# Four units to a burst, PSUM in three double slots and two single banks, and an earlier x: a fused attention and channel-mix kernel

## The chip, the cores and the metric

The kernel runs on one core of a Trainium2 chip. TensorE (PE) multiplies matrices into PSUM, VectorE (DVE), ScalarE (ACT) and GpSimd (POOL) work on tiles, and SyncE (SP) issues transfers. Each engine takes its instructions in the order in which they are written and waits for the others by semaphores. The metric is the time of one execution on the device, in microseconds; of several runs the median counts. Inputs are those of the reference, except that the channel mix's weights and factors arrive as float64.

## The reference

Two pieces follow each other on x of shape (4, 12608, 128). First an attention through 32 inducing points: the points attend to all of x, which gives h (32 rows for each batch), and each row of x attends to h. Then a channel mix, with d_ff = 1024, in which each row is mixed with the row before it:

```python
def mab(q, kv):
    s = scale * (q @ kv.transpose(0, 2, 1))
    s = s - s.max(-1, keepdims=True)
    a = np.exp(s)
    a /= a.sum(-1, keepdims=True) + 1e-09
    return a @ kv
h = mab(I, x)
x = mab(x, h)
...
x_prev = np.concatenate([np.zeros((B, 1, D)), x[:, :-1, :]], axis=1)
xk = mu_k * x + (1.0 - mu_k) * x_prev
xr = mu_r * x + (1.0 - mu_r) * x_prev
k = np.maximum(xk @ w_k, 0.0)
v = k * k @ w_v
r = 1.0 / (1.0 + np.exp(-(xr @ w_r)))
out = r * v
```

## The kernel before

**Tiling.** A batch is cut into six blocks of 2048 tokens and a tail of 320, a block into four groups of 512 tokens; with the tail's, a batch has 25 groups. A group's 1024 channels of d_ff are cut into four units of 256. So there are 100 groups and 400 units, and the main loop goes through them, one unit to an iteration. The second attention's normalised weights (not its output rows) stand in `R`, as a high and a low part, and the kernel multiplies them with `h @ w_k` and `h @ w_r`, made once for each batch by `combine`; so the up product of a unit has an inner length of 64 and runs as pairs of half-height matmuls.

**One unit.** `up` (six half-height matmuls in three pairs, L792) fills a double slot of PSUM. `square` then takes relu on VectorE (L802, to `k_t`), the square rounded to `kh` on ScalarE (L807), or on VectorE for the units of the set `high_vector` (L804), the full square on ScalarE (L808), and the rest `kl` as a difference on GpSimd (L810). `down` (L821) multiplies `kh` and `kl` with `w_v` in six full-height matmuls, four units later (`LAG`). Once a group, `zgate` (L780) makes the sigmoid gate, `gate` (L826) multiplies, `store` (L837) transposes and sends out.

**The other stages.** Between the units stand the steps of the attention. `stage_a` brings one block of the next batch through the first attention: transposes on VectorE (L344) whose parts SP copies into place (L347), scores, maximum, exponentials, their transpose (L420), sums (L430) and a product with x (`hmm`, L441), added to a running sum (L456). `stage_b` brings the next block of this batch through the second: scores (L621), maximum, exponentials, total (L642, L643), reciprocal (L646), multiplication (L649), a transpose back (L655, L657), a high and a low part (L667), and copies into `R`. `head` does the whole first attention of batch 0, while the float64 weights are converted on the chip (`load_weight`); `start` does the second attention of its first four groups.

**What sets the order.** The order is written by hand. Steps are hung on iterations by `at(n, f)` (run at the end of iteration n) and `soon(n, f)` (run after the up products of iteration n), with offsets from the start `s` of a segment of twelve iterations, that is three groups, in which one block of each stage is done. Ups are issued for two units at once, at every second iteration.

**PSUM.** Eight banks of 2 KB a partition: the pool `pa` has two slots of two banks (up products), `pv` two banks (down and gate products), `pb` two single banks, named a and b, that all the steps of the attention share.

Of the kernel before, what the change touches and what calls it, by code (L numbers as in the profile page):

```python
# [19 lines left out]
def kernel(  # L20
# [40 lines left out]
    pa = ctx.enter_context(tc.tile_pool(name="pa", bufs=2, space=bass.MemoryType.PSUM))  # L61
    pv = ctx.enter_context(tc.tile_pool(name="pv", bufs=2, space=bass.MemoryType.PSUM))
    pb = ctx.enter_context(tc.tile_pool(name="pb", bufs=1, space=bass.MemoryType.PSUM))
    banks = iter("ab" * 64)

    def pb_tile(bank=None):

        return pb.tile([P, G], F32, name="pb_" + (bank or next(banks)))
# [16 lines left out]
    def load_weight(dst, src, n, raw):  # L85
# [11 lines left out]
        def steps():  # L97
# [36 lines left out]
            return [exponent, mantissa, clamp, sign, low, power]  # L134
# [3 lines left out]
    tp = pb_tile()  # L138
# [75 lines left out]
    def stage_a_head(j):  # L214
# [10 lines left out]
        def tr():  # L225
            for h in range(0, Q, 2):
                ps = pa.tile([P, 2, G], F32, name="ps_a")
# [21 lines left out]
        def scores():  # L249
            L.s1 = pv.tile([P, G], F32, name="ps_v")  # L250
# [26 lines left out]
        def etrans():  # L277
            L.ep = pb_tile()
# [14 lines left out]
        def hmm():  # L293
            ps = L.hp = pb_tile()
# [31 lines left out]
    def stage_a(b, j, at, t):  # L326
# [30 lines left out]
        def t_scores():  # L357
            ps = pb_tile("b")
            for i in range(Q):
                nc.tensor.matmul(out=ps[M * i:M * (i + 1), :tw], lhsT=indT, rhs=S.xt[jt, i],  # L360
                                 start=True, stop=True)
            s1 = sm.tile([P, tw], F32, name="s1", bufs=1)
            nc.vector.tensor_copy(out=s1, in_=ps[:, :tw])
# [4 lines left out]
        def scores():  # L368
            ps = pb_tile("a")
            L["s1"] = ps  # L370
            for i in range(Q):
                nc.tensor.matmul(out=ps[M * i:M * (i + 1), :], lhsT=indT, rhs=S.xt[j, i],  # L372
                                 start=True, stop=True)
            mx = sm.tile([P, 1], F32, name="mx1", bufs=4)
            nc.vector.tensor_reduce(out=mx, in_=ps, op=ALU.max, axis=AX.X)
# [46 lines left out]
        def t_etrans():  # L422
            ps = pb_tile("b")
# [36 lines left out]
        for c in range(Q):  # L460
            at(t + ((-1, 0, 1, 3) if (b, j) != (1, 0) else (4, 5, 6, 7))[c], lambda c=c: btr(c))
        if tail:
            at(t + 5, t_tr)
            soon(t + 11, t_scores)
        at(t + 9, scores)
        at(t + 10 + tail, common)
        at(t + 11 + tail, running)
        at(t + 15, expo)
        at(t + 17, etrans)
        if tail:  # L470
            at(t + 17, t_etrans)
        at(t + 18, sums)
        at(t + 18, lambda: hmm(0))
        at(t + 18, lambda: hmm(1))
        at(t + 18, t_hmm)
        at(t + 20, acc)
        k = order_a.index((b, j))
        for bn, jn in order_a[k + 1:]:
            if jn < NBLK - 1:
                at(t + 8, lambda: load_x(bn, jn))  # L480
# [5 lines left out]
    def combine(b, at=None, t=0):  # L486
# [3 lines left out]
        def maxes():  # L490
            bank = next(banks)
            ps = pb_tile(bank)
# [3 lines left out]
            ps2 = pb_tile(bank)  # L496
# [19 lines left out]
        def weights_sum():  # L516
            ws, wt = L["ws"], L.get("wt")
            ps = pb_tile(None if ahead else "b")
# [51 lines left out]
        at(t + 8, weights)  # L570
        at(t + 9, hfin)
        for gate in range(2):
            prod, high, low = wpart(gate, lambda: pb_tile("a"))
            at(t + 10 + 2 * gate, prod)
            at(t + 10 + 2 * gate, high)
            at(t + 11 + 2 * gate, low)
# [26 lines left out]
    def stage_b(b, j, at, t, bank="b", direct=False, offsets=(0, 1, 1, 2, 3, 5, 5, 6, 6, 7, 9)):  # L603
# [80 lines left out]
        for n, f in zip(offsets, (scores, trans, maxi, sub, expo, total, recip, mult, back, high, low)):  # L684
            at(t + n, f)
# [9 lines left out]
    def stage_b_first(g):  # L695
# [7 lines left out]
        def scores():  # L703
            ps = L["ps"] = pb_tile("abaa"[g])
# [7 lines left out]
        def diff():  # L712
# [7 lines left out]
            mx = L["ps"][:, n * M:n * M + n]  # L720
            nc.vector.tensor_reduce(out=mx, in_=s2, op=ALU.max, axis=AX.X)
# [355 lines left out]
```

## Time and profile before

| | us |
|---|---|
| median of 3 runs | 1127.31 |
| lowest, highest | 1123.52, 2022.45 |
| the profiled run | 1123.31 |
| its span | 1121.5 |

The profile shows the profiled run alone; a span leaves out what lies before the first and after the last instruction, 1.8 us here. The granted clock of TensorE over the span is 0.99. Stages by the end of their last gate in the trace: the head and the first five groups end at 138.2 us, the first batch at 360.8, the second at 623.6, the third at 885.8. A window's row gives busy time of each engine between two such marks; an engine whose busy time comes up to the window's length bounds it. In a timeline's row the start comes first, then the duration, the engine, the line and the operation; a bracket at its end is the idle time before it and what ended that. Matmuls are pipelined, so a matmul's own duration is longer than what it adds; the step from one start to the next tells that.

### The profile page before, as it was taken

The numbers are of one execution on the slowest core, as the hardware profiler recorded it, in microseconds if no ns is written. First come the engines' busy times: TensorE is split into PE (matmuls) and PEld (weight loads), VectorE is DVE, ScalarE is ACT, GpSimd is POOL, SyncE is SP. The second block draws the span as 40 slices with busy tenths as digits, with TensorE's granted clock in tenths as the row PEclk, the third lists the DMA queues.
The fourth block names the chain that finished last, engine by engine and source line by source line (L and its number), as shares of the span: only waits on it lengthen the run. The fifth ranks groups of instructions, "written<-read, shape, count | busy, mean of one in ns | idle before, by whom it ended". The sixth has DMA issues, their size and how long they took to land.

```text
span 1121.5 us, 19356 instructions
## 1 busy us (share of the span) xinstructions
PE 1077.1 (96%) x6610; PEld 736.2 (66%) x6610; DVE 913.1 (81%) x1301; ACT 962.4 (86%) x1101; POOL 948.3 (85%) x421
## 2 busy tenths in 40 slices
PE   5779899999999999999999999999999999999997
PEld 4546566666676666666766666667667666667775
DVE  5677789998678999998777899998776788888665
ACT  5486688898998988898998898999899989999995
POOL 2157599888888999888888998889889899999996
PEclk9999899999999999999999999999999999999998
DMA  9204575675327656757317646765414424453422
GB/s 274 77 1 119 115 155 135 146 175 133 60 39 164 138 133 144 169 134 158 60 29 139 156 109 154 162 157 114 86 31 94 91 48 95 87 97 71 88 38 35
DMA packets 267634, 123.61 MB, mean 110 GB/s; under 512 B 225648, under 2 KB 247056, under 8 KB 265232
## 3 DMA queue, kind: packets, MB, share of 16 engines
q1 hardware_dynamic: 267200, 122.35, 50.7%
q8 instruction: 53, 0.87, 0.3%
q14 instruction: 45, 0.37, 0.1%
q10 hardware_dynamic: 336, 0.02, 0.0%
HBM read 28.07 MB, written 25.82 MB: 48 GB/s over the span
## 4 chain that ended last, share of the span: by engine, by line
PE 84%; DVE 6%; SPq 4%; ACT 3%; issue 1%; DMA 1%; POOL 1%; DVEq 0%; ACTq 0%
PE ps_v L821 48%; PE ps_a L792 26%; PE ps_v L780 4%; DVE k_t L802 2%; PE pb_b L621 2%; PE pb_a L441 2%; PE pb_a L372 2%; DMA xb<-in_x_dram 1%; SPq L95 1%; ACT kh L807 1%; SPq L193 1%; SPq L601 1%; ACT k_t L808 1%; POOL kl L810 1%; DVE kh L804 1%
## 5 line engine op out<-in xcount | busy, mean ns | idle before, releaser
L810 POOL TENSOR_TENSOR kl<-k_t,kh 128x1024 fp32r<-128x1024 f32 (+2 forms) x400 | 936.6, 2381 | 135.9 <-ACT k_t L808 124.9
L802 DVE TENSOR_SCALAR k_t<-ps_a 128x1024 f32<-128x1024 f32 (+1 forms) x400 | 476.8, 1198 | 86.3 <-PE ps_a L792 64.4
L808 ACT ACTIVATE k_t<-k_t 128x1024 f32<-128x1024 f32 (+1 forms) x400 | 418.0, 1048 | 50.3 <-DVE kh L804 16.9
L807 ACT ACTIVATE kh<-k_t 128x1024 fp32r<-128x1024 f32 (+1 forms) x352 | 365.3, 1038 | 67.2 <-DVE k_t L802 66.7
L792 PE MATMUL ps_a<-R,W 64*128 64x512 f32 (+1 forms) x2400 | 332.1, 408 | 8.8 <-DVE k_t L802 7.0
L792 PEld LDWEIGHTS ps_a<-R,W 64*128 64x128 f32 x2400 | 209.4, 186 | 131.1 <-issue 52.4
L821 PE MATMUL ps_v<-kh,wvh 128*128 128x512 f32 (+1 forms) x800 | 272.3, 422 | 0.0
L821 PE MATMUL ps_v<-kl,wvh 128*128 128x512 f32 (+1 forms) x800 | 249.8, 393 | 1.7 <-POOL kl L810 1.2
L821 PE MATMUL ps_v<-kh,wvl 128*128 128x512 f32 (+1 forms) x800 | 249.9, 394 | 0.0
L821 PEld LDWEIGHTS ps_v<-kh,wvh 128*128 128x128 f32 x800 | 132.7, 189 | 95.2 <-issue 38.5
L821 PEld LDWEIGHTS ps_v<-kl,wvh 128*128 128x128 f32 x800 | 150.4, 189 | 37.6 <-POOL kl L810 2.2
L821 PEld LDWEIGHTS ps_v<-kh,wvl 128*128 128x128 f32 x800 | 150.3, 189 | 33.7
L826 DVE TENSOR_TENSOR oT<-ps_v,rT 128x512 f32<-128x512 f32 (+1 forms) x100 | 66.9, 669 | 25.0 <-PE ps_v L821 24.8
L780 PE MATMUL ps_v<-R,Wg 128*128 128x512 f32 (+1 forms) x200 | 64.2, 402 | 6.4 <-DVE oT L826 6.4
L837 DVE STREAM_TRANSPOSE ot<-oT 128x512 f32<-128x512 f32 x96 | 67.0, 698 | 0.0
L804 DVE SCALAR_TENSOR_TENSOR kh<-ps_a,k_t 128x1024 fp32r<-128x1024 f32 x48 | 58.8, 1225 | 1.7
L782 ACT ACTIVATE rT<-ps_v 128x512 f32<-128x512 f32 (+1 forms) x100 | 57.9, 579 | 0.3
L344 DVE STREAM_TRANSPOSE xs<-xb 128x512 f32<-128x512 f32 x72 | 49.9, 693 | 10.0 <-DMA xb<-in_x_dram 5.5
L780 PEld LDWEIGHTS ps_v<-R,Wg 128*128 128x128 f32 x200 | 37.2, 192 | 17.2 <-DVE oT L826 8.5
L782 ACT ACT_TABLE_LOAD x31 | 39.8, 1283 | 0.5
L667 DVE TENSOR_TENSOR hl<-pb_b,hl 128x512 fp32r<-128x512 f32 x23 | 15.9, 690 | 14.2 <-ACT hl L664 13.9
L621 PE MATMUL pb_b<-xt,hT 128*32 128x512 f32 x184 | 24.4, 603 | 0.6 <-DVE R L753 0.6
(217 smaller groups left out, 528.7 us busy)
## 6 DMA issues: line engine op xcount, KB each, us to landing
out_dram<-ot SPq DMA_DIRECT2D x184, 128.0 KB, 3.3
R<-R SPq DMA_DIRECT2D x88, 256.0 KB, 3.2
xb<-in_x_dram SPq DMA_DIRECT2D x18, 1024.0 KB, 5.8
xt<-xs SPq DMA_DIRECT2D x288, 64.0 KB, 2.0
R<-hl SPq DMA_DIRECT2D x96, 128.0 KB, 2.4
R<-hl SPq DMA_DIRECT2D x96, 127.8 KB, 2.4
kh<-in_x_dram SPq DMA_DIRECT2D x4, 512.0 KB, 7.9
kl<-in_x_dram SPq DMA_DIRECT2D x4, 512.0 KB, 7.5
```

Source lines behind the costliest of these rows:

```text
L344: nc.vector.transpose(out=xs.rearrange("p (s q) -> p s q", q=M), in_=S.xb[j][:, :, M * c:M * (c + 1)])
L780: nc.tensor.matmul(out=ps[:, :w], lhsT=S.Wg, rhs=R[:, s, :w], start=(s == 0), stop=(s == 1))
L782: nc.scalar.activation(out=self.rT, in_=ps[:, :w], func=AF.Sigmoid)
L792: nc.tensor.matmul(out=ps[:, r, :w], lhsT=S.W[a][rows, u * P:(u + 1) * P], rhs=R[rows, k, :w], start=(n == 0), stop=(n == 2))
L802: nc.vector.tensor_scalar(out=k, in0=ps, scalar1=0.0, scalar2=None, op0=ALU.max)
L804: nc.vector.scalar_tensor_tensor(out=kh, in0=ps, scalar=0.0, in1=k, op0=ALU.max, op1=ALU.mult)
L807: nc.scalar.activation(out=kh, in_=k, func=AF.Square)
L808: nc.scalar.activation(out=k, in_=k, func=AF.Square)
L810: return lambda eng, a, z: eng.tensor_tensor(out=kl[:, :, a:z], in0=k[:, :, a:z], in1=kh.bitcast(F32)[:, :, a:z], op=ALU.subtract)
L821: nc.tensor.matmul(out=self.v, lhsT=wt[:, fc, :], rhs=kk[:, c, :], start=(fc == 0 and n == 0), stop=(fc == FC - 1 and n == 2))
L826: nc.vector.tensor_tensor(out=self.oT, in0=self.v, in1=self.rT, op=ALU.mult)
L837: nc.vector.transpose(out=ot[:, o:o + w], in_=self.oT)
```

## The change

**PSUM.** `pa` has three double slots, `pv` one bank, `pb` one bank. A step that asked for bank a of `pb` now takes a whole double slot, and so does `zgate`; the down product has the one `pv` bank.

**Bursts.** The ups of a whole group come together at its first iteration: three, then the `soon` steps of that iteration, then the fourth. Groups 1 and 2 keep bursts of two. `kl` has five buffers, it had four. `high_vector` holds one unit of a segment, it held two.

**The attention's steps.** Stage A's steps are hung on iterations 3 to 15 of a segment instead of −1 to 20, stage B's start five iterations before the segment instead of one after it, and the combine's come four to six iterations earlier.

**Head and start.** On SP's queue, six blocks' loads of x stand ahead of or between the weights in another order. The conversion of weights has no separate step for the sign. Eight small matmuls (`warm`) come in after the first transposes; the matmuls of `spin` come after the sum of the weights, three instead of ten. The steps of the first four groups' attention are hung on other iterations, and in finer pieces.

```diff
-    pa = ... bufs=2 ...
-    pv = ... bufs=2 ...
+    pa = ... bufs=3 ...
+    pv = ... bufs=1 ...
     pb = ... bufs=1 ...
...
-    def pb_tile(bank=None):
-        return pb.tile([P, G], F32, name="pb_" + (bank or next(banks)))
+    def pb_tile(bank):
+        if bank == "a":
+            return pa_tile()[:, 0, :]
+        if bank == "v":
+            return pv_tile()
+        return pb.tile([P, G], F32, name="pb_b")
...
-            at(t + ((-1, 0, 1, 3) if (b, j) != (1, 0) else (4, 5, 6, 7))[c], lambda c=c: btr(c))
+            at(t + 3 + c, lambda c=c: btr(c))
...
         at(t + 9, scores)
-        at(t + 10 + tail, common)
-        at(t + 11 + tail, running)
-        at(t + 15, expo)
-        at(t + 17, etrans)
+        at(t + 10, maxi)
+        at(t + 10, common)
+        at(t + 10, running)
+        soon(t + 11, expo)
+        at(t + 12, etrans)
...
-        at(t + 18, sums)
-        at(t + 18, lambda: hmm(0))
-        at(t + 18, lambda: hmm(1))
-        at(t + 18, t_hmm)
-        at(t + 20, acc)
+        at(t + 13, sums)
+        at(t + 13, lambda: hmm(0))
+        at(t + 13, lambda: hmm(1))
+        at(t + 15, t_hmm)
+        at(t + 14 + tail, acc)
...
-    def stage_b(..., offsets=(0, 1, 1, 2, 3, 5, 5, 6, 6, 7, 9)):
+    def stage_b(..., offsets=(0, 1, 2, 3, 4, 5, 5, 6, 6, 7, 8)):
...
-            at(t + n, f)
+            (soon if f in (expo, high) else at)(t + n, f)
...
         def zgate(self):
-            ps = self.v = pv.tile([P, G], F32, name="ps_v")[:, :w]
+            ps = pb_tile("a")[:, :w]
...
-            kl = mp.tile([P, UC, G], F32R, name="kl", bufs=4)
+            kl = mp.tile([P, UC, G], F32R, name="kl", bufs=5)
...
-            high_vector |= {s + 4, s + 8}
+            high_vector.add(s + 5)
...
-                stage_b(b, j + 1, at, s - 2 if j == (b == 0) else s + 1)
+                stage_b(b, j + 1, at, s - 5)
...
+    bursts = {n: units[n:n + NU] for n in range(0, len(units), NU)}
+    for n in range(NU, 3 * NU, 2):
+        bursts[n] = units[n:n + 2]
...
-                if n % 2 == 0:
-                    for g, v in units[n:n + 2]:
-                        g.up(v)
+                burst = bursts.get(n, [])
+                for g, v in burst[:3]:
+                    g.up(v)
                 run(early.pop(n, []))
+                for g, v in burst[3:]:
+                    g.up(v)
```

TensorE's order around the product of stage A (`hmm`), in the first segment of batch 0 that has one beside a full second attention. Names ending in numbers are buffers: `ps_a` a double slot, `pb_a` the bank a, `ps_v` a `pv` bank. Before, with a burst of two units just ending:

```order
L792 MATMUL ps_a_1852<-R_1564,W0_718 128x512 x2
L792 MATMUL ps_a_1852<-R_1564,W1_719 128x512 x2
L792 MATMUL ps_a_1852<-R_1564,W0_718 128x512 x2
L821 MATMUL ps_v_1710<-kh_1753,wvh_111 128x512 x2
L821 MATMUL ps_v_1710<-kh_1753,wvl_112 128x512 x2
L821 MATMUL ps_v_1710<-kl_1754,wvh_111 128x512 x2
L441 MATMUL pb_a_1873<-xb_1180,e1_1843 32x128 x16
L821 MATMUL ps_v_1710<-kh_1769,wvh_111 128x512 x2
L821 MATMUL ps_v_1710<-kh_1769,wvl_112 128x512 x2
L821 MATMUL ps_v_1710<-kl_1770,wvh_111 128x512 x2
L792 MATMUL ps_a_1911<-R_1595,W0_718 128x512 x2
```

After; three other ups, nine rows like the first three here, stand right ahead of these:

```order
L813 MATMUL ps_a_2075<-R_1540,W0_710 128x512 x2
L813 MATMUL ps_a_2075<-R_1540,W1_711 128x512 x2
L813 MATMUL ps_a_2075<-R_1540,W0_710 128x512 x2
L842 MATMUL ps_v_2089<-kh_1958,wvh_111 128x512 x2
L842 MATMUL ps_v_2089<-kh_1958,wvl_112 128x512 x2
L842 MATMUL ps_v_2089<-kl_1959,wvh_111 128x512 x2
L801 MATMUL ps_a_2109<-R_1540,Wg_712 128x512 x2
L842 MATMUL ps_v_2089<-kh_1976,wvh_111 128x512 x2
L842 MATMUL ps_v_2089<-kh_1976,wvl_112 128x512 x2
L842 MATMUL ps_v_2089<-kl_1977,wvh_111 128x512 x2
L452 MATMUL ps_a_2123<-xb_1593,e1_2096 32x128 x16
L842 MATMUL ps_v_2089<-kh_2006,wvh_111 128x512 x2
```

The product has moved from a bank of its own into a double slot, and so has the gate's (L780 before, two iterations ahead of the rows shown, into a `ps_v`; L801 after); what stood between two bursts of two units now stands behind one burst of four.

VectorE's order at the same place, from the exponentials' transpose on. Before:

```order
L420 STREAM_TRANSPOSE e1_2225<-e1t_2155 128x512
L802 TENSOR_SCALAR k_t_2242<-ps_a_2228 128x1024
L430 TENSOR_SCALAR sum_1404<-sum_1404,alpha_2157,ss_2156 128x1
L642 TENSOR_REDUCE pb_b_2106<-s2_2139 128x16
L643 TENSOR_SCALAR sm2_2273<-pb_b_2106 128x16
L646 RECIPROCAL pb_b_2106<-sm2_2273 128x16
L802 TENSOR_SCALAR k_t_2277<-ps_a_2235 128x1024
L649 TENSOR_TENSOR s2_2139<-s2_2139,pb_b_2106 128x512
L657 STREAM_TRANSPOSE pb_b_2106<-s2_2139 128x512
L826 TENSOR_TENSOR oT_2292<-ps_v_2082,rT_2085 128x512
L802 TENSOR_SCALAR k_t_2308<-ps_a_2294 128x1024
```

After, from the first relu of the burst (`ps_a_2054`) to behind stage A's sum:

```order
L823 TENSOR_SCALAR k_t_2082<-ps_a_2054 128x1024
L431 STREAM_TRANSPOSE e1_2096<-e1t_2029 128x512
L654 TENSOR_REDUCE pb_b_1922<-s2_1973 128x16
L655 TENSOR_SCALAR sm2_2098<-pb_b_1922 128x16
L658 RECIPROCAL pb_b_1922<-sm2_2098 128x16
L823 TENSOR_SCALAR k_t_2102<-ps_a_2061 128x1024
L858 STREAM_TRANSPOSE ot_2114<-oT_2052 128x512
L441 TENSOR_SCALAR sum_1267<-sum_1267,alpha_2031,ss_2030 128x1
L661 TENSOR_TENSOR s2_1973<-s2_1973,pb_b_1922 128x512
L669 STREAM_TRANSPOSE pb_b_1922<-s2_1973 128x512
L823 TENSOR_SCALAR k_t_2145<-ps_a_2068 128x1024
L467 SCALAR_TENSOR_TENSOR acc_1266<-acc_1266,alpha_2031,ps_a_2123 128x128
```

The total and the reciprocal of the second attention (L642 to L646 before, L654 to L658 after) now stand between the first and the second relu of one burst, the store, the sum, the multiplication and the transpose back between its second and its third.

SP's queue in the head. `kh` and `kl` are buffers borrowed for blocks of x, `k_t` and `oT` for raw weights. Before:

```order
L201 DMA xl_113<-in_x_dram 80x4x128
L95 DMA k_t_115<-in_moe_w_k_dram 128x1024
L193 DMA kh_117<-in_x_dram 128x8x128
L193 DMA kh_119<-in_x_dram 128x8x128
L95 DMA k_t_121<-in_moe_w_k_dram 128x1024
L193 DMA kh_123<-in_x_dram 128x8x128
L193 DMA kh_125<-in_x_dram 128x8x128
L95 DMA k_t_127<-in_moe_w_v_dram 128x4x256
L193 DMA kl_129<-in_x_dram 128x8x128
L193 DMA kl_131<-in_x_dram 128x8x128
L95 DMA k_t_133<-in_moe_w_v_dram 128x4x256
```

After:

```order
L208 DMA xl_113<-in_x_dram 80x4x128
L200 DMA kh_115<-in_x_dram 128x8x128
L200 DMA kh_117<-in_x_dram 128x8x128
L200 DMA kh_119<-in_x_dram 128x8x128
L200 DMA kh_121<-in_x_dram 128x8x128
L106 DMA k_t_123<-in_moe_w_k_dram 128x1024
L200 DMA kl_125<-in_x_dram 128x8x128
L200 DMA kl_127<-in_x_dram 128x8x128
L106 DMA k_t_129<-in_moe_w_k_dram 128x1024
L200 DMA kl_131<-in_x_dram 128x8x128
L200 DMA kl_133<-in_x_dram 128x8x128
L106 DMA k_t_135<-in_moe_w_v_dram 128x4x256
```

The tail (`xl`) and the first two blocks of x, two loads each, stand ahead of every weight, and each weight has moved back by two blocks.

More of the change, by code (lines that the diff above doesn't have):

```diff
@@ L490, in maxes @@
         def maxes():
-            bank = next(banks)
-            ps = pb_tile(bank)
+            ps = pb_tile("a")
             nc.tensor.transpose(out=ps[:1, :P], in_=S.mrun, identity=ident)
@@ L728, in norm @@
             s2 = L["s2"]
-            tot = L["ps"][:, n * M:n * M + n]
+            if g in (1, 2):
+                tot = L["mx"]
+                L["pt"] = pb_tile("va"[g - 1])
+            else:
+                slot = pa_tile()
+                tot, L["pt"] = slot[:, 1, :n], slot[:, 0, :]
             sm2 = sm.tile([P, Q * Q], F32, name="sm2")[:, :n]
@@ L755, in idle @@
         def idle(k):
-            ps = pa.tile([P, 2, G], F32, name="ps_a")
+            ps = pa_tile()
             for i in range(k):
                 nc.tensor.matmul(out=ps[:, 1, :], lhsT=ident, rhs=S.x0, start=True, stop=True)
-        return scores, diff, expo, norm, turn, high, low, idle
+        return scores, trans, maxi, sub, expo, norm, turn, high, low, idle
     NG = (NBLK - 1) * Q + 1
@@ L898, in spin, with warm @@
     def spin(n):
-        half = P // 2
-        ps = pa.tile([P, 2, G], F32, name="ps_a")
+        ps = pa_tile()
         rhs = wvh.rearrange("p c d -> p (c d)")[:, :G]
-        for i in range(3):
+        for i in range(n):
             nc.tensor.matmul(out=ps[:, i % 2, :], lhsT=wvh[:, i, :], rhs=rhs, start=True, stop=True)
+    def warm(n):
+        ps = pa_tile()
         for i in range(n):
-            for r in range(2):
-                rows = slice(half * r, half * (r + 1))
-                nc.tensor.matmul(out=ps[:, r, :], lhsT=wvh[rows, (i + r) % FC, :], rhs=rhs[rows],
-                                 start=True, stop=True)
-        for i in range(3):
-            nc.tensor.matmul(out=ps[:, i % 2, :], lhsT=wvh[:, i, :], rhs=rhs, start=True, stop=True)
-    PARTS_FIRST = 6
-    PARTS = ((0, 0, 0), (3, 3, 0), (3, 3, 0), (3, 3, 0), (3, 3, 1), (1, 0, 0), (0, 0, 0))
+            nc.tensor.matmul(out=ps[:, i % 2, :P], lhsT=ident, rhs=ident, start=True, stop=True)
+    PARTS = ((0, 0), (3, 2), (3, 2), (3, 2), (3, 2), (5, 2), (0, 0))
     def head():
         last = NBLK - 1
-        for k in range(2):
-            ab[k].tr()
-        place(PARTS_FIRST)
+        ab[0].tr()
+        warm(8)
+        ab[1].tr()
         ab[0].scores()
@@ L934, in head @@
                 ab[k - 1].acc()
+                ab[k - 1].sums()
             if k == 0:
```

140 lines of the change are left out of this document (76 added, 64 removed).

## The prediction

> **What bounds the kernel now.** I read the busy times first, then windows by stage, then the timelines of TensorE and VectorE inside a steady stage. The columns of the windows are length, then busy time with the number of instructions of PE, PEld, DVE, ACT and POOL, then the granted clock, the DMA share and GB/s.
>
> ```profile
> PE 1077.1 (96%) x6610; PEld 736.2 (66%) x6610; DVE 913.1 (81%) x1301; ACT 962.4 (86%) x1101; POOL 948.3 (85%) x421
> 0.00:49.00 49.00, 33.79 (x405) 23.60 (x405) 29.38 (x85) 25.66 (x61) 11.63 (x21) 1.00 0.72 200
> 49.00:138.20 89.20, 74.30 (x481) 47.59 (x482) 67.20 (x108) 59.81 (x69) 52.37 (x22) 0.90 0.32 71
> 360.80:623.60 262.80, 260.78 (x1590) 177.41 (x1587) 225.02 (x321) 235.99 (x265) 234.82 (x100) 1.00 0.57 125
> 885.80:1121.50 235.70, 227.33 (x1206) 160.05 (x1202) 179.06 (x202) 205.73 (x220) 217.91 (x94) 0.99 0.40 74
> 405.50:437.50 32.00, 32.00 (x200) 21.49 (x199) 29.80 (x43) 28.74 (x33) 28.43 (x13) 1.00 0.64 148
> 955.00:984.60 29.60, 29.60 (x158) 20.45 (x158) 24.99 (x29) 27.23 (x30) 28.24 (x13) 1.00 0.48 90
> 1050.00:1088.00 38.00, 38.00 (x199) 26.94 (x198) 24.28 (x24) 35.03 (x37) 38.00 (x18) 1.00 0.31 55
> ```
>
> The rows show three regimes. In a steady segment of three groups (405.5 to 437.5) TensorE is busy for all 32.0 us, so whatever it saves there shortens the segment, and whatever it waits for lengthens it. The cover beneath it is thin: VectorE 29.8, ScalarE 28.7, GpSimd 28.4 us. In the last four groups of the last batch (1050 to 1088) GpSimd is full as well, 38.0 us, or 9.5 us a group, and TensorE can't go below that. The first 138 us are no steady state: in the second window TensorE idles 89.2 − 74.3 = 14.9 us and its clock is 0.90, which costs up to 8.9 us more.
>
> **The change, part by part. Fewer changes of matmul form.** The up products run on half-height tiles, everything else on full height.
>
> ```profile
> 507.57 0.62 PE L821 MATMUL ps_v<-kl,wvh 128*128 128x512 f32 x2
> 508.12 1.66 PE L792 MATMUL ps_a<-R,W 64*128 64x512 f32 x12
> 509.71 0.73 PE L821 MATMUL ps_v<-kh,wvh 128*128 128x512 f32 x2
> 510.27 0.63 PE L821 MATMUL ps_v<-kh,wvl 128*128 128x512 f32 x2
> 510.74 0.63 PE L821 MATMUL ps_v<-kl,wvh 128*128 128x512 f32 x2
> ```
>
> A pair of full matmuls takes 510.74 − 510.27 = 0.47 us, so one streams in 0.233. From 507.57 to 510.27 stand two pairs and six double half-tiles, 2 × 0.467 + 6 × 0.233 = 2.33 us; 2.70 passed. The excess 0.37 is the price of two changes of form, 0.185 to 0.19 each. After the head the order counts 515 such changes before and 338 after, since a burst now takes four units instead of two. 177 × 0.19 = −33.6 us.
>
> **The fourth up of a burst.** There are three double slots of PSUM, so the fourth up takes the slot of the group's first unit and must wait for its relu (L823 after, L802 before).
>
> ```profile
> 57.16 1.22 DVE L802 TENSOR_SCALAR k_t<-ps_a 128x1024 f32<-128x1024 f32 x1
> 58.43 0.96 PE L792 MATMUL ps_a<-R,W 64*128 64x512 f32 x6 [0.41 <-DVE k_t L802]
> 509.20 1.22 DVE L802 TENSOR_SCALAR k_t<-ps_a 128x1024 f32<-128x1024 f32 x1 [0.28 <-PE ps_a L792]
> ```
>
> The relu starts 509.20 − 508.12 = 1.08 us after the burst's first matmul and runs 1.21, to 2.28. A waiting up starts 58.43 − 58.38 = 0.05 us after a relu, at 2.34; three ups end at 0.09 + 9 × 0.233 = 2.19. With some 0.10 us to refill the array this is +0.24 us in each of 97 four-unit bursts, +23.3 us. Bounds: 0 if the relu came sooner, which its own 1.08 us forbid, and +0.41, the wait in the row, in each, +40.
>
> **The gate product and stage A's product.** The gate product (L801) leaves the pool of single banks and takes a double slot, that of the second unit; stage A's product (L452) takes that of the third. Both now wait for relus which VectorE reaches only after the attention steps ahead of them. What one of these steps takes is read from start to start.
>
> ```profile
> 446.63 1.21 DVE L802 TENSOR_SCALAR k_t<-ps_a 128x1024 f32<-128x1024 f32 x1
> 447.87 1.23 DVE L804 SCALAR_TENSOR_TENSOR kh<-ps_a,k_t 128x1024 fp32r<-128x1024 f32 x1
> 449.01 1.21 DVE L802 TENSOR_SCALAR k_t<-ps_a 128x1024 f32<-128x1024 f32 x1
> 450.14 0.70 DVE L837 STREAM_TRANSPOSE ot<-oT 128x512 f32<-128x512 f32 x1
> 450.76 0.67 DVE L420 STREAM_TRANSPOSE e<-e1t 128x512 f32<-128x512 f32 x1
> 451.36 1.18 DVE L802 TENSOR_SCALAR k_t<-ps_a 128x1024 f32<-128x1024 f32 x1
> 452.47 0.25 DVE L430 TENSOR_SCALAR sum<-sum,alpha,ss 128x1 f32<-128x1 f32 x1
> 452.64 0.68 DVE L642 TENSOR_REDUCE pb_b<-s 128x16 f32<-128x512 f32 x1
> 453.36 0.17 DVE L643 TENSOR_SCALAR sm<-pb_b 128x16 f32<-128x16 f32 x1
> 453.56 0.26 DVE L646 RECIPROCAL pb_b<-sm 128x16 f32<-128x16 f32 x1
> 453.74 1.21 DVE L802 TENSOR_SCALAR k_t<-ps_a 128x1024 f32<-128x1024 f32 x1
> 454.86 0.67 DVE L649 TENSOR_TENSOR s<-s,pb_b 128x512 f32<-128x512 f32 x1
> 455.56 0.73 DVE L655 STREAM_TRANSPOSE pb_b<-s 128x512 f32<-128x512 f32 x1
> 456.20 0.67 DVE L826 TENSOR_TENSOR oT<-ps_v,rT 128x512 f32<-128x512 f32 x1
> ```
>
> The steps are: relu 1.13, store transpose 0.62, exponentials' transpose 0.60, sum 0.17, total 0.72, its epsilon 0.20, reciprocal 0.18, multiply 0.70, transpose back 0.64, relu ahead of a square 1.24. I walk the new VectorE order from the burst's start. In the group with stage A's product: first relu 1.07, then 1.13 + 0.60 + 0.72 + 0.20 + 0.18 put the second relu at 3.90, ending 5.11; the gate product, which TensorE reaches at 4.72 (four ups, one change, one unit's down of 1.40), starts near 5.15: +0.43, with the refill +0.53. Then 1.13 + 0.62 + 0.17 + 0.70 + 0.64 put the third relu at 7.16, ending 8.37; stage A's product, due at 5.25 + 0.47 + 1.40 + 0.19 = 7.3, waits to 8.4: with the refill +1.2. In the next group, where VectorE also squares the second unit, its relu starts at 1.07 + 1.13 + 0.62 = 2.82 and its square ends at 2.82 + 1.24 + 1.23 = 5.29: gate +0.64, with the refill +0.74. By the order, 12 groups have the full first case and 18 the second; three have only the tail's attention beside stage A (+0.3). Sum: 12 × 0.53 + 18 × 0.74 = +19.7 and 12 × 1.2 + 3 × 0.3 = +15.3 us. Such a wait is seen now at a few places:
>
> ```profile
> 355.49 0.97 PE L792 MATMUL ps_a<-R,W 64*128 64x512 f32 x6 [1.40 <-DVE k_t L802]
> 352.00:358.00 6.00, 4.25 (x23) 2.67 (x22) 5.97 (x7) 4.39 (x6) 6.00 (x3) 1.00 0.48 108
> ```
>
> For both waits the ends are nothing (VectorE early) and 33 × 1.4 + 33 × 0.41 = +60, the two waits shown; the walk's 35 lies between, nearer the middle than either end. What stands behind them on TensorE is the next units' down products; they and all later steps move by the same amount.
>
> **What is hidden.** Squares that VectorE gives up (24, order) go to ScalarE at 1.04 us (the row below), +25 us over four batches, about 1.04 in a segment where it has 32.0 − 28.7 = 3.3 free. A fifth kl buffer frees nothing that waits; GpSimd's work is the same, and it holds the last batch: there segments go from 29.8 only to about 29.4, which the sums above, counted as if TensorE bound, overstate by a few us. The combine's steps, moved four iterations earlier, cost +0.5 in all, an estimate by the wait it adds before three gate products. Stage A's transposes come three to four iterations later, and with them 16 copies a block on SP's queue, among the doublings and stores that stand there; the scores that need them come three iterations after the last (3 × 2.67 us, 32.0 over 12), and a copy lands in 2.0, so it stays hidden; if SP's queue were 6 us late, the scores would wait.
>
> ```profile
> xt<-xs SPq DMA_DIRECT2D x288, 64.0 KB, 2.0
> L807 ACT ACTIVATE kh<-k_t 128x1024 fp32r<-128x1024 f32 (+1 forms) x352 | 365.3, 1038 | 67.2 <-DVE k_t L802 66.7
> L792 PE MATMUL ps_a<-R,W 64*128 64x512 f32 (+1 forms) x2400 | 332.1, 408 | 8.8 <-DVE k_t L802 7.0
> ```
>
> **The start.** x goes ahead of the weights on SP's queue, five sign operations go, the spin stands behind the weights' sum, and the first groups' attention is interleaved anew.
>
> ```profile
> 8.80 3.71 PE L230 MATMUL ps_a<-ident,kh 128*128 128x128 f32 x16 [4.47 <-DMA kh<-in_x_dram]
> 83.98 1.15 PE L744 MATMUL pb_a<-ident,aT 128*64 128x128 f32 x16 [3.02 <-DVE aT L734]
> 113.72 1.22 PE L780 MATMUL ps_v<-R,Wg 128*128 128x512 f32 x2 [3.74 <-DVE oT L826]
> 128.12 0.73 PE L780 MATMUL ps_v<-R,Wg 128*128 128x512 f32 x2 [2.15 <-DVE oT L826]
> 105.00:120.00 15.00, 11.26 (x49) 7.51 (x46) 8.51 (x14) 7.31 (x9) 7.66 (x4) 0.77 0.73 168
> ```
>
> The first wait, 4.5 us, is for an x block behind weights in the queue; it goes. The next three, 8.9 us, stand at places that the new order unties. Half of the clock's 8.9 us goes with them, 4.5. Together −18. The lower end is the first wait alone, about −5; the upper is all idle time and clock loss of the window, −24, and the weights, now later, may take some back.
>
> Sum: −33.6 + 23.3 + 19.7 + 15.3 + 0.5 − 18 = +7.2 on the span of 1121.5: 1128.7, and with the 1.8 us around it (1123.31 − 1121.5) 1130.5 us. The profiled run is 4 us under the median of 1127.3.
>
> **The rivals.** One: the waits for the second and third relu don't bite, because VectorE runs ahead of my walk, and only the fourth up waits. For it: ups wait 7.0 us in all for relus now, in the row L792. Against: the order sets the second relu behind five attention steps. Time 1130.5 − 35 = 1095.5, faster.
>
> Two: the start yields only the load order's 5 us, since its attention chain is the same work on VectorE. For it: 67.2 of 89.2 us busy there. Time 1130.5 + 13 = 1143.5.
>
> Three, the other side: the repeated waits drop the clock. In the window of 105 to 120 a wait of 3.74 us stands with a granted clock of 0.77, 3.45 us lost in 15. A drop of about 3.4 us at half speed loses 1.7 us; in each of the 12 to 15 groups with both waits, 20 to 25 us: 1153, slower. It decides from the length of idle time in such a stretch: 3.74 dropped it, the 1.75 idle us of 352 to 358 left it at 1.00, and mine come to 0.53 + 1.2 = 1.73 in some 3.5. The Trainium skill, "TensorE: Matmul & The Clock Gate", section "A second HAM failure mode: psum-queue depth-cycling", speaks for this one: it says that short idling between matmul groups, as PSUM slots cycle, makes the clock swing between half and full. By that rule the same 1153; the 1.40 us wait above at clock 1.00 doesn't bear it out.
>
> **How the numbers follow.** A measurement of this kernel tells about 2% from no change: under 1104.8 or over 1149.9 against 1127.3. Chances: my sum 0.39 (its own range 1110 to 1149), rival one 0.32, rival two 0.13, rival three 0.16. Faster: 0.32 and a little of the first, 0.33. Slower: most of the third, a quarter of the second and a little of the first, 0.20. Same: 0.47. The range runs from rival one with a start of −24 (1089.5, taken as 1090) to a little past rival three, 1155.
>
> **What would show it.** The number of up runs halves, and a change still costs 0.19. The row of up products has idle time before it ended by the relu (L823), some 0.13 us a group; L801 waits for L823 or L825, 0.4 to 0.7 us in the groups named; L452 waits 1.2 us. A segment of three groups takes 33 to 34.3 us where it took 32.0, one of the last batch 29.4, and the first four groups end near 120 instead of 138. If L801 and L452 show no wait, rival one is right; if the clock falls under 1.00 in steady segments, rival three. The sum is wrong if VectorE's steps overlap or wait otherwise than start to start in the present trace.

## The result, and the profile after

| | before | after |
|---|---|---|
| median | 1125.5 us | 1184.5 us |
| profiled span | 1121.5 us | 1185.5 us |
| granted clock over the span | 0.99 | 0.979 |

The change makes the kernel slower: the ratio is 1.0527, with a 95% interval from 1.0500 to 1.0554. The forecast was 1130.5 us, no measurable change, with 1155 as the upper end of its range. One of the four runs of the kernel before took 2022.45 us, the others 1123.5 to 1127.3; the ratio leaves it out.

The same page after: busy times first, then the chain of waits by engine. Before, that row read as the last line here.

```profile
PE 1095.8 (92%) x6619; PEld 750.6 (63%) x6619; DVE 878.3 (74%) x1272; ACT 985.5 (83%) x1125; POOL 945.9 (80%) x421
PE 61%; DVE 20%; ACT 6%; issue 4%; POOL 1%; DMA 0%; DVEq 0%; ACTq 0%; POOLq 0%
```

```profile
PE 84%; DVE 6%; SPq 4%; ACT 3%; issue 1%; DMA 1%; POOL 1%; DVEq 0%; ACTq 0%
```

TensorE no longer fills its span, and VectorE's share of the chain rises from 6% to 20%: TensorE waits for it. The windows, cut at the same marks as before (the fifth group's gate and the ends of the batches), then a steady segment, a segment of the last batch, and the groups around a combine:

```profile
132.60:371.80 239.20, 224.65 (x1343) 152.14 (x1347) 183.39 (x268) 203.98 (x230) 194.98 (x84) 0.99 0.52 114
371.80:654.50 282.70, 266.14 (x1591) 180.20 (x1590) 217.69 (x313) 242.10 (x271) 233.91 (x101) 0.99 0.53 115
937.70:1185.50 247.80, 229.14 (x1214) 164.92 (x1213) 168.36 (x195) 209.74 (x224) 218.84 (x95) 0.98 0.37 69
419.50:454.40 34.90, 32.69 (x202) 21.61 (x200) 28.57 (x42) 29.58 (x34) 28.41 (x13) 1.00 0.57 131
985.00:1016.70 31.70, 29.78 (x159) 20.84 (x158) 23.54 (x29) 28.47 (x31) 28.52 (x13) 1.00 0.30 59
560.00:600.00 40.00, 36.10 (x220) 24.31 (x219) 24.68 (x38) 30.15 (x33) 28.61 (x13) 0.91 0.22 42
```

A batch takes 282.7 us where it took 262.8. A steady segment is 34.9 us long with 2.2 us of TensorE idle (32.0 before, none idle). A segment of the last batch went from 29.8 to 31.7. Around a combine the clock falls to 0.91. By stretches the 64.0 us of span are: the start up to the fifth gate −5.6 (132.6 against 138.2), the rest of batch 0 +16.6, batch 1 +19.9, batch 2 +21.0 (283.2 against 262.2), the last batch and the end +12.1.

TensorE's waits, summed by the line that waits and the one that ends the wait (total us, times, longest):

```profile
PE ps_a L801 <- DVE kh L825: 19.6, 23, 0.9
PE ps_a L801 <- DVE k_t L823: 14.4, 18, 3.5
PE ps_a L452 <- DVE k_t L823: 13.4, 15, 1.1
PE ps_a L813 <- DVE k_t L823: 11.0, 11, 1.4
PE ps_v L842 <- DVE oT L847: 4.5, 1, 4.5
```

These are the gate product, stage A's product, the up products and the down product. Before, the ups waited 7.0 us for relus in all. Two groups of a steady segment show how it comes about:

```profile
418.99 3.37 PE L813 MATMUL ps_a<-R,W 64*128 64x512 f32 x24
424.21 0.73 PE L801 MATMUL ps_a<-R,Wg 128*128 128x512 f32 x2 [0.26 <-DVE k_t L823]
427.44 1.08 PE L452 MATMUL ps_a<-xb,e 128*32 128x128 f32 x32 [1.10 <-DVE k_t L823]
431.44 3.32 PE L813 MATMUL ps_a<-R,W 64*128 64x512 f32 x24
434.69 0.73 PE L842 MATMUL ps_v<-kh,wvh 128*128 128x512 f32 x2
437.20 0.73 PE L801 MATMUL ps_a<-R,Wg 128*128 128x512 f32 x2 [0.85 <-DVE kh L825]
443.06 3.32 PE L813 MATMUL ps_a<-R,W 64*128 64x512 f32 x24
```

From one burst (L813) to the next are 12.45 and 11.62 us. Within them stand the waits that the prediction named, in their places: 0.26 us for the second relu, 1.10 for the third, and 0.85 for VectorE's square, where the walk, without the refill, had 0.43, 1.1 and 0.64.

### The profile page after: what moved, and what is told of

Read it like the earlier page. It is cut to its first block, busy times and chain, and to the rows that moved or that the text cites. A ratio compares the mean times of both kernels' runs of the same rounds, so it can differ in the third digit from the quotient of the medians.

```text
span 1185.5 us, 19423 instructions
## 1 busy us (share of the span) xinstructions
PE 1095.8 (92%) x6619; PEld 750.6 (63%) x6619; DVE 878.3 (74%) x1272; ACT 985.5 (83%) x1125; POOL 945.9 (80%) x421
## 4 chain that ended last, share of the span: by engine, by line
PE 61%; DVE 20%; ACT 6%; issue 4%; POOL 1%; DMA 0%; DVEq 0%; ACTq 0%; POOLq 0%
PE ps_v L842 34%; PE ps_a L813 18%; DVE k_t L823 10%; PE ps_a L801 4%; DVE kh L825 3%; PE pb_b L633 2%; ACT kh L828 2%; PE ps_a L381 1%; PE ps_a L452 1%; POOL kl L831 1%; ACT L803 1%; ACT k_t L829 1%; DVE ot L858 1%; DVE pb_b L654 1%; DVE oT L847 1%
## 5 line engine op out<-in xcount | busy, mean ns | idle before, releaser
L823 DVE TENSOR_SCALAR k_t<-ps_a 128x1024 f32<-128x1024 f32 (+1 forms) x400 | 473.4, 1192 | 55.5 <-PE ps_a L813 39.9
L828 ACT ACTIVATE kh<-k_t 128x1024 fp32r<-128x1024 f32 (+1 forms) x376 | 390.5, 1038 | 90.7 <-DVE k_t L823 81.5
L813 PE MATMUL ps_a<-R,W 64*128 64x512 f32 (+1 forms) x2400 | 333.0, 409 | 18.5 <-DVE k_t L823 11.0
L813 PEld LDWEIGHTS ps_a<-R,W 64*128 64x128 f32 x2400 | 210.8, 186 | 141.6 <-DVE k_t L823 53.8
L842 PE MATMUL ps_v<-kh,wvh 128*128 128x512 f32 (+1 forms) x800 | 268.7, 418 | 4.5 <-DVE oT L847 4.5
L842 PEld LDWEIGHTS ps_v<-kh,wvh 128*128 128x128 f32 x800 | 140.5, 192 | 85.2 <-issue 47.5
L847 DVE TENSOR_TENSOR oT<-ps_v,rT 128x512 f32<-128x512 f32 (+1 forms) x100 | 67.9, 679 | 79.6 <-PE ps_v L842 79.6
L801 PE MATMUL ps_a<-R,Wg 128*128 128x512 f32 (+1 forms) x200 | 68.0, 422 | 34.0 <-DVE kh L825 19.6
L801 PEld LDWEIGHTS ps_a<-R,Wg 128*128 128x128 f32 x200 | 34.6, 192 | 56.1 <-DVE kh L825 29.6
L803 ACT ACTIVATE rT<-ps_a 128x512 f32<-128x512 f32 (+1 forms) x100 | 57.9, 579 | 0.3
L386 DVE TENSOR_REDUCE mx<-ps_a 128x1 f32<-128x512 f32 x18 | 12.5, 692 | 37.3 <-PE ps_a L381 37.3
L825 DVE SCALAR_TENSOR_TENSOR kh<-ps_a,k_t 128x1024 fp32r<-128x1024 f32 x24 | 29.4, 1224 | 14.2 <-PE ps_v L842 14.1
L452 PE MATMUL ps_a<-xb,e 128*32 128x128 f32 x576 | 19.5, 276 | 13.4 <-DVE k_t L823 13.4
```

The costliest lines, as they stand in the source:

```text
L801: nc.tensor.matmul(out=ps[:, :w], lhsT=S.Wg, rhs=R[:, s, :w], start=(s == 0), stop=(s == 1))
L803: nc.scalar.activation(out=self.rT, in_=ps[:, :w], func=AF.Sigmoid)
L813: nc.tensor.matmul(out=ps[:, r, :w], lhsT=S.W[a][rows, u * P:(u + 1) * P], rhs=R[rows, k, :w], start=(n == 0), stop=(n == 2))
L823: nc.vector.tensor_scalar(out=k, in0=ps, scalar1=0.0, scalar2=None, op0=ALU.max)
L825: nc.vector.scalar_tensor_tensor(out=kh, in0=ps, scalar=0.0, in1=k, op0=ALU.max, op1=ALU.mult)
L828: nc.scalar.activation(out=kh, in_=k, func=AF.Square)
```

## The experiments

The first run set the theory that bursts of four bring the waits against another, the next two took the combine and the head by themselves; three more separated PSUM from the order of the steps; the last five took single waits out, and then all of them. Theories A and B mean something of their own in each run; C to F are explained where they first stand. A ratio is to the kernel before, with its 95% interval.

**Bursts of two again, everything else as changed.**

```diff
-    bursts = {n: units[n:n + NU] for n in range(0, len(units), NU)}
-    for n in range(NU, 3 * NU, 2):
+    bursts = {n: units[n:n + NU] for n in range(0, NU, NU)}
+    for n in range(NU, len(units), 2):
         bursts[n] = units[n:n + 2]
```

> The changed kernel with bursts of two units, as before, from group 1 on; PSUM, the attention's steps, head and start stay as changed. Theory A (the time comes from TensorE waiting for slots that only a relu frees, which bursts of four bring): the waits ahead of the gate product (L801, 34 us in sum after) and ahead of stage A's product (L452, 13 us) nearly vanish, the one of 3.5 us at each batch's combine too, and with it the half clock there; a steady segment of three groups falls from 34.9 to 32.0 to 32.6 us, the time to 1115 to 1135. Rival B (the steps' new places and one single bank fewer cost by themselves): segments stay at 34 or more, the time at 1165 or more.

Measured 1187.3 us, ratio 1.0569 (1.0547 to 1.0590). Theory A fell. The waits that it names do vanish (neither L801 nor L452 waits any more, and the clock around a combine is 1.00), but the time stays: others take their place. TensorE's largest are now

```profile
PE ps_a L813 <- DVE k_t L823: 24.1, 22, 1.5
PE ps_a L813 <- ACT rT L803: 16.7, 19, 3.6
PE ps_v L842 <- DVE oT L847: 10.6, 11, 4.8
```

The ups themselves wait for the sigmoid (L803), which holds the gate product's double slot, and for relus; the down product waits for the gate (L847), which holds the only bank of its pool. Plain groups of the last batch take 9.61 us, as before, against 9.50 with bursts of four.

**The combine one iteration later.**

```diff
-        at(t + 4, weights)
-        at(t + 5, hfin)
+        at(t + 5, weights)
+        at(t + 7, hfin)
```

The two weight products move from 6 and 10 to 8 and 12.

> The changed kernel with the combine's weights one iteration later (5 instead of 4), h and the weight products two later. Theory A (the reciprocal of the sum stands ahead of the second unit's relu on VectorE and waits for a matmul behind a down product; the gate product waits 3.5 us and the clock then stays at half for some 7 us, 3.6 us lost): both go at three places, 3 x 7 = 21 us, to about 1163. Rival B (the wait only moves to the next relu): the time stays within 6 us of 1184.

Measured 1185.3 us, ratio 1.0554 (1.0522 to 1.0586): no gain. The 3.5 us wait of the gate product is gone (the longest is now 0.5 us for L823), but the next batch's scores (L633) wait 2.6 us for h, and gate products wait up to 1.4 us for the weights' low parts. The clock of that region is 0.96, not 1.00. The rival held: the wait moved.

**The changed head in the kernel before.** The edit is the head's part of the change: load order, no sign step, `warm`, `spin` behind the weights' sum.

> The kernel before with the changed head alone (x ahead of the weights, no sign step, warm matmuls, spin of three behind the weights' sum). Theory A (the head ends at nearly the same time, 48.3 after against 49.3 before for the first product with h, since conversion and exponentials set it; the shorter spin leaves the clock at half for some us after): within 5 us of 1125, the head's end earlier by 0 to 2 us. Rival B (the load order is worth what the first wait for x showed, 4.5 us, and more with the sign steps): 1117 to 1121, head's end at 45 or sooner.

Measured 1121.2 us, ratio 0.9972 (0.9959 to 0.9984). The first product with h starts at 47.7 us (49.3 before), the fifth gate at 136.1 (138.2). It is 3.6 us less than the kernel before beside it (1124.8), the only version here that is under it, though by less than the 2% that would count as faster. Theory A's two numbers hold (within 5 us, the head's end up to 2 us sooner) and rival B's head's end doesn't. Theory A's clock does not hold: it stays at 0.99 between 36 and 60 us, so the lower clock that the changed kernel shows there (0.79) isn't the head's doing alone. What brings it is open.

**The steps alone, in the kernel before.** The offsets of stage A, stage B and the combine, `high_vector`, the earlier x of the second batch; PSUM, bursts, head and start as before. The tail's transpose of exponentials takes a double slot, since bank a is occupied at its new time.

```diff
-        at(t + 18, lambda: hmm(0))
+        at(t + 13, lambda: hmm(0))
...
-                stage_b(b, j + 1, at, s - 2 if j == (b == 0) else s + 1)
+                stage_b(b, j + 1, at, s - 5)
```

> The kernel before with the attention's steps alone at their new places (stage A, stage B, combine, one square on VectorE a segment), PSUM, bursts, head and start as before. Theory C (the gate product and stage A's steps take double slots out of the rotation of the up products, so each waits for the relus of ups that hold the other slots, whatever the burst): a segment stays near 32 us, time 1115 to 1135. Theory D (the packed steps cost by themselves: VectorE gets to its relus late, and the combine has no room): segments of 33.5 us or more, the combine's groups as long as after (17.5), time 1155 or more. Half of it in each: 1135 to 1155.

Measured 1133.9 us, ratio 1.0078 (1.0063 to 1.0093), inside theory C's range at its upper end. Segments take 32.5 us and more: at some places stage A's scores (L374) wait for copies of transposed x on their way through SP's queue. Their weight loads idle 11.6 us in all until such a copy lands, 0.2 before and 0.9 in the changed kernel. So the prediction's claim that these copies stay hidden holds in the changed kernel, and not with the steps alone.

**PSUM alone, in the kernel before.**

```diff
-    pa = ... bufs=2 ...
-    pv = ... bufs=2 ...
+    pa = ... bufs=3 ...
+    pv = ... bufs=1 ...
...
-        return pb.tile([P, G], F32, name="pb_" + (bank or next(banks)))
+        if (bank or next(banks)) == "a":
+            return pa.tile([P, 2, G], F32, name="ps_a")[:, 0, :]
+        return pb.tile([P, G], F32, name="pb_b")
...
         def zgate(self):
-            ps = self.v = pv.tile([P, G], F32, name="ps_v")[:, :w]
+            ps = pa.tile([P, 2, G], F32, name="ps_a")[:, 0, :w]
```

> The kernel before with the new PSUM alone: three double slots, one bank for the down product, one single bank; the gate product and what asked for bank a take a double slot. Bursts of two, steps, head and start as before. Theory C: up products wait for the sigmoid and for relus, segments 33.5 us or more, time 1155 to 1190. Theory D: no new waits, 1120 to 1135.

Measured 1186.1 us, ratio 1.0540 (1.0522 to 1.0559). With the steps where they were and bursts of two, PSUM's new division costs as much as the whole change. Its waits (ups are L794 here, the gate product L782, the down product L823) and a steady segment:

```profile
PE ps_a L794 <- ACT rT L784: 20.1, 27, 2.7
PE ps_v L823 <- DVE oT L828: 20.0, 12, 5.4
PE ps_a L782 <- ACT e1t L411: 9.4, 11, 1.1
PE ps_a L782 <- DVE kh L806: 6.9, 15, 0.5
```

```profile
400.00:435.06 35.06, 33.00 (x200) 21.10 (x198) 30.13 (x42) 28.77 (x32) 28.91 (x13) 1.00 0.45 104
```

Three sharings appear by name: the gate's slot stands in the ups' way (20.1), the single down bank holds the next group until the gate has read it (20.0), and stage A's scores keep a double slot until their exponentials (9.4). No run gives back one of the three alone, so how they share the 61 us is told by these waits only.

**PSUM and bursts of four, steps as before.** As the last, with the changed kernel's bursts from the fourth group on.

> As before_newpsum, with bursts of four units from the fourth group on. By the sums for plain groups the bursts themselves give 0.1 us a group; theory C: within 10 us of before_newpsum, the gate product waiting in place of the ups. If bursts of four are the cause of the waits: 20 us or more above it.

Measured 1367.2 us, ratio 1.2157 (1.2137 to 1.2177), 181 us above the run before it, so theory C's 10 us are missed by far. Bursts of four need the new steps: with the old ones the ups wait 125 us for VectorE's relus and squares and 40 us for stage A's exponentials. With the new ones they cost and gain nothing that can be told (1187.3 against 1184.5). So the four corners, with bursts of two, are: neither 1125, steps 1134, PSUM 1186, both (with the new head and start) 1187. That the last two agree doesn't make them the same waits: with the new steps the ups wait longest for relus (24.1 us, against 2.7 with the old steps). The like totals may be chance.

**Six kh buffers, four kl buffers.** The same space, one buffer moved; six and five don't fit (the pool would take 74 KB a partition, and 71.6 are left).

```diff
-            kh = ... name="kh", bufs=5 ...
-            kl = ... name="kl", bufs=5 ...
+            kh = ... name="kh", bufs=6 ...
+            kl = ... name="kl", bufs=4 ...
```

> The changed kernel with six kh buffers and four kl buffers instead of five and five. Theory A (in the group where VectorE squares the second unit, its square waits for a down product to free a kh buffer, 0.46 us in the first three batches and 1.04 in the last): the gate product's wait there falls from 0.85 to 0.4 us, 23 times: -8 to -12, to about 1174. Rival B (four kl buffers make relus or ScalarE wait, or the place of the square alone decides): 1180 or more.

Measured 1173.4 us, ratio 1.0432 (1.0414 to 1.0450), 11 us less than the changed kernel. The gate product's wait in that group falls from 0.85 to 0.53 us. VectorE's square (L825), which waited 14.1 us in all for down products to free a buffer, no longer waits for one. Theory A of this run holds: the buffer that the change gave to kl was needed by kh.

**The combine spread out, with the next block behind it.** Weights at 5, h at 7, products at 9 and 13, the block at 11.

```diff
-        at(t + 4, weights)
-        at(t + 5, hfin)
+        at(t + 5, weights)
+        at(t + 7, hfin)
...
-            at(t + 6 + 4 * gate, prod)
+            at(t + 9 + 4 * gate, prod)
...
-            stage_b(b + 1, 0, at, s + 7)
+            stage_b(b + 1, 0, at, s + 11)
```

> The changed kernel with the combine's weights at 5, h at 7, the products at 9 and 13 and the next batch's first second-attention block at 11 (it was 4, 5, 6, 10 and 7). Theory E (each of these steps needs its own room between a matmul that VectorE waits for and a slot that TensorE waits for; one iteration later alone gave nothing because h and the scores behind it were still at their heels): 3 x 6 us less, 1164 to 1170, the clock there 1.00. Rival (the region is short of VectorE or ScalarE time, so the wait moves on again): 1178 or more.

Measured 1176.5 us, ratio 1.0472 (1.0454 to 1.0489): 8 us less, under half of what was expected, and the clock of the region is 1.00 again. From gate to gate the long group goes from 17.5 to 12.2 us, but two groups behind it are longer by 0.5 and 1.9 us, and ups wait more for relus (L813 by L823, 16.2 us in all instead of 11.0).

**Stage A's product one iteration later.**

```diff
-        at(t + 13, lambda: hmm(0))
-        at(t + 13, lambda: hmm(1))
+        at(t + 14, lambda: hmm(0))
+        at(t + 14, lambda: hmm(1))
...
-        at(t + 14 + tail, acc)
+        at(t + 15, acc)
```

> The changed kernel with stage A's product one iteration later (14 instead of 13, its sum at 15 everywhere). Theory C: the wait of 1.1 us for the third unit's relu is over by then; 15 x (1.1 + 0.1 to refill) = -18, to 1166 to 1172. Rival (the slot goes back later, and the next burst's ups wait instead): 1178 or more.

Measured 1172.7 us, ratio 1.0431 (1.0407 to 1.0455): 12 us less and just above theory C's range. From gate to gate the group goes from 12.0 to 10.9 us, as expected; in each tail block a new wait of up to 1.5 us for the sigmoid takes some of it back.

**The second attention's low part one iteration later.**

```diff
-    def stage_b(..., offsets=(0, 1, 2, 3, 4, 5, 5, 6, 6, 7, 8)):
+    def stage_b(..., offsets=(0, 1, 2, 3, 4, 5, 5, 6, 6, 7, 9)):
```

> The changed kernel with the second attention's low part one iteration later (offset 9 instead of 8, except in the first block), behind the gate and the first relu of a burst instead of ahead of them. Theory F (in the last batch VectorE waits 1.75 us for ScalarE there and the fourth up 1.06 us for the relu behind it): 4 to 5 of these and 3 at the batches' starts vanish, -6 to -9, to 1176 to 1179. Rival (the relu of the second unit comes later by the 0.7 us of that step, and the gate product waits for it): 1182 or more.

Measured 1177.2 us, ratio 1.0470 (1.0442 to 1.0498): 7 us less, inside theory F's range. The ups' waits for L823 fall from 11.0 to 2.6 us. The rival has a small part: the gate product's waits for VectorE's square (L825) rise from 19.6 to 23.0.

**All of these together**, and two more: VectorE's square at the group's fourth unit, and bank b for the last group's down product. The next batch's first block, now later, keeps its low part at offset 8.

```diff
-            high_vector.add(s + 5)
+            high_vector.add(s + 7)
...
-                self.v = pv_tile()[:, :w]
+                self.v = (pb_tile('b') if self.b == B - 1 and self.g == NG - 1 else pv_tile())[:, :w]
```

> All together in the changed kernel: six kh and four kl buffers, the combine apart, stage A's product and the low part one iteration later, VectorE's square at the fourth unit of its group instead of the second, and bank b for the last group's down product. If the waits add up as the single ones do: 1184.5 - 11 (measured) - 18 - 18 - 8 - 9 (gate product, 23 x 0.4) - 6 (the end: 4.5 us of wait and some of its half clock) = 1115, range 1108 to 1125, steady segments near 32. If waits only move: 1140 or more.

Measured 1127.5 us, ratio 1.0037 (1.0026 to 1.0049), 57 us less than the changed kernel, and 2.5 above the range for waits that add up. The four single gains sum to 38; the other 19 go with the two last edits or with waits that had moved when one alone was taken out, and how they divide isn't shown. The waits left are small, and a steady segment is 32.6 us:

```profile
PE ps_a L813 <- DVE k_t L823: 7.7, 13, 1.4
PE ps_a L801 <- DVE k_t L823: 4.2, 15, 0.6
```

```profile
400.00:432.63 32.63, 32.09 (x198) 21.41 (x197) 28.34 (x41) 29.21 (x33) 28.23 (x13) 1.00 0.61 128
```

So with three double slots and bursts of four, 57 of the 59 us go when steps are moved, one buffer goes from kl to kh, and one product of the last group gets bank b. What these edits aim at are waits for shared slots and buffers, with the half clock behind the longest. What is left is 0.4% over the kernel before: the fewer changes of form and the earlier x don't quite pay for what remains.

## Why the prediction was wrong

**Right: the change of form and the fourth up.** The terms −33.6 and +23.3 make −0.1 us a group. Plain groups of the last batch went from 9.61 to 9.50 us, and back to 9.61 with bursts of two. GpSimd works without a pause there (32 units in 75.78 us, 9.47 a group), so these groups could hardly have gained more and don't prove the two terms alone. The fourth up can be read by itself: from the burst at 431.44 to the down product at 434.69 are 3.25 us. Without the 2.80 us of four ups and the 0.19 that a burst of two takes there beyond its ups (508.12 to 509.71 before), 0.26 are left, where the prediction had 0.24.

**Right in mechanism, somewhat small: the waits of the gate product and of stage A's product.** The walk gave up to 34.3 us for a segment; 34.9 was measured. It missed that VectorE's square also needs a free kh buffer, which a down product gives back 0.46 us late in the steady segments:

```profile
435.92 1.22 DVE L825 SCALAR_TENSOR_TENSOR kh<-ps_a,k_t 128x1024 fp32r<-128x1024 f32 x1 [0.46 <-PE ps_v L842]
```

The prediction weighed a fifth kl buffer and didn't count kh's: with four units in flight and one being made, five are just full, and a burst puts four ups ahead of the down product that frees one. The run with six gave 11 us. The walk also priced 18 groups with such a square; 23 wait in the trace, six of them in the last batch, which it had left out.

**Wrong: "the combine's steps ... cost +0.5 in all".** Each of the three combines costs a wait of up to 3.5 us and then half clock. The one of the second batch:

```profile
572.53 0.28 PE L531 MATMUL pb_b<-sum,stack 128*128 128x1 f32 x2
576.28 1.19 PE L801 MATMUL ps_a<-R,Wg 128*128 128x512 f32 x2 [3.47 <-DVE k_t L823]
577.27 1.05 PE L842 MATMUL ps_v<-kh,wvh 128*128 128x512 f32 x2
578.12 1.05 PE L842 MATMUL ps_v<-kh,wvl 128*128 128x512 f32 x2
```

```profile
572.85 0.16 DVE L533 TENSOR_SCALAR rd<-pb_b 128x1 f32<-128x1 f32 x1 [2.77 <-PE pb_b L531]
573.24 1.76 DVE L540 TENSOR_SCALAR mk<-stack,rd 128x32 f32<-128x32 f32 x1
574.92 1.21 DVE L823 TENSOR_SCALAR k_t<-ps_a 128x1024 f32<-128x1024 f32 x1
```

The reciprocal's steps stand on VectorE ahead of the second unit's relu and wait for a matmul that TensorE reaches only behind a down product (2.77 us idle); then the step to `mk` takes 1.76 us where it took 0.51 before; then comes the relu, and then the gate product. Pairs of matmuls that follow each other in 0.47 us take 0.85 (578.12 − 577.27), and the window of 40 us has a clock of 0.91, 3.6 us lost. The wait and the clock make 7 us, three times 21, as an estimate. Spreading the steps brought only 8 of them back, since ups further on then wait longer; why they do was not followed up. (By the diff the combine's weights, h and first product come four iterations earlier, its second product two, not four to six as said ahead of the prediction.)

**Wrong: the last batch.** The prediction let it go to 29.4 us a segment, on the ground that GpSimd bounds it. It takes 31.7, and GpSimd is busy for 28.5 of them, so it bounds nothing there. The mechanism is the one that was walked for the other batches and not for this one: without stage A VectorE is early, waits for ScalarE in front of the low part, and the first relu of the burst stands behind that.

```profile
990.26 0.69 DVE L679 TENSOR_TENSOR hl<-pb_b,hl 128x512 fp32r<-128x512 f32 x1 [1.75 <-ACT hl L676]
991.47 2.35 DVE L823 TENSOR_SCALAR k_t<-ps_a 128x1024 f32<-128x1024 f32 x2
994.85 1.23 DVE L825 SCALAR_TENSOR_TENSOR kh<-ps_a,k_t 128x1024 fp32r<-128x1024 f32 x1 [1.04 <-PE ps_v L842]
```

```profile
992.73 0.96 PE L813 MATMUL ps_a<-R,W 64*128 64x512 f32 x6 [1.06 <-DVE k_t L823]
996.13 0.73 PE L801 MATMUL ps_a<-R,Wg 128*128 128x512 f32 x2 [0.85 <-DVE kh L825]
```

The fourth up waits 1.06 us instead of 0.24, and the gate product 0.85 for VectorE's square, which waits 1.04 for a kh buffer. Moving the low part gave 7 us over the run.

**Wrong: the end.** No term stood for the single down bank. The last group's first down product waits for the gate of the group before, which on VectorE stands behind its shares of the last `kl`:

```profile
1166.02 4.12 DVE L831 TENSOR_TENSOR kl<-k_t,kh 128x320 fp32r<-128x320 f32 x1 [0.92 <-ACT k_t L829]
1173.80 0.87 PE L842 MATMUL ps_v<-kh,wvh 128*128 128x320 f32 x2 [4.46 <-DVE oT L847]
```

The kernel before has the same step, and it takes 4.35 us there; but with a second bank the last group's down products start without waiting for that gate.

**Wrong: the start, −18.** Measured −5.6. The three waits that were to go are gone by their names, but others stand in their stead: ups (L813) wait 8.4 us between 49 and 133 us, for VectorE and ScalarE, where they waited 3.3. In all TensorE idles 11.7 us there instead of 14.9. The clock there is hardly better (0.92 against 0.90). The head alone is worth 3.6 us, near the 4.5 us of the first wait. This was rival two: it put 5 us on the start.

**Rival three** was right for a few places and not for those it meant. The clock fell where TensorE idled 3.47 us at a stretch, at the combines, and at the end (4.46 us). It didn't where it idled 0.26 and 1.10 us within 3.3 us (the steady segment above has 1.00, with both). Where it fell, the loss was 3.6 us in the 40 us around a combine, twice the 1.7 us that the rival put on a drop. The rule on slots that cycle, of the Trainium skill's "TensorE: Matmul & The Clock Gate", section "A second HAM failure mode: psum-queue depth-cycling", isn't borne out by these repeated short waits.

**The sum.** Beside the start, the terms came to +25.2 us and 69.6 were measured. The failed step is the list of what the new slots make wait: the waits of two instructions in two kinds of groups were priced, and the same sharing at the combine, in the last batch, at the end and in kh's buffers was taken for nothing or, at the combine, for 0.5. The single runs put 8 us on the combine (of an estimated 21), 7 on the low part, 11 on kh's buffers and 12 on stage A's product, which was priced; all edits together take 57 out. The prediction saw rightly that these waits come from products in double slots. It walked them for bursts of four alone; the runs show that PSUM's new division costs as much with bursts of two.

## What to carry to other kernels

When short-lived tiles move into a rotating pool of big slots, each allocation can make its writer wait for the reader of the slot as many allocations back as the pool has slots, three here, and that reader may stand behind anything on its own engine. So the new order is to be walked in every kind of stretch, ramps and seams included, and not in the steady one alone. A kernel whose bounding engine is at 100% has nothing to pay such waits with; one slot or buffer given to the wrong pool can cost more than the saving it was moved for.

## What the runs showed of the hardware

Two VectorE instructions took as long as GpSimd was at work beside them. One is the step to `mk`, 128x32:

```profile
567.91 7.06 POOL L831 TENSOR_TENSOR kl<-k_t,kh 128x1024 fp32r<-128x1024 f32 x3 [1.11 <-PE ps_a L460]
```

After, it took 1.76 us and ended at 575.00, when GpSimd's subtraction ended (574.97). Before, it took 0.51:

```profile
552.96 2.40 POOL L810 TENSOR_TENSOR kl<-k_t,kh 128x1024 fp32r<-128x1024 f32 x1 [1.34 <-ACT k_t L808]
554.89 0.51 DVE L528 TENSOR_SCALAR mk<-stack,rd 128x32 f32<-128x32 f32 x1
```

It ended at 555.40, GpSimd's at 555.36. In the head, with GpSimd idle, a like step takes 0.30.

The other is the subtraction of 128x320 on VectorE at the end. It took 4.12 us while GpSimd had four of its own one after another, and 0.47 a little later, with GpSimd idle. In the kernel before it took 4.35 us:

```profile
1092.72 17.49 POOL L810 TENSOR_TENSOR kl<-k_t,kh 128x1024 fp32r<-128x1024 f32 x9
1106.21 4.35 DVE L810 TENSOR_TENSOR kl<-k_t,kh 128x320 fp32r<-128x320 f32 x1
```

Both times it ended 0.35 us after GpSimd's last.

The Trainium skill, "GPSIMD Engine Reference", says in its section "1. Specifications" that GpSimd's interfaces to SBUF are shared with VectorE, in contention with instructions that read two SBUF inputs or run in a two-port mode. The trace agrees for the subtraction, which reads two; the step to `mk` reads one, and no run here shows in which mode it ran. Relus that read PSUM kept their 1.2 us beside a busy GpSimd (568.86 to 570.08).
